# Float64 weights to float32 in an attention and mixture-of-experts kernel: one more ScalarE pass, one fewer VectorE pass, half of the residuals moved from GpSimd to VectorE

## The chip, the cores and the metric

The kernel runs on one core of a Trainium2 chip. The metric is the device time of one execution in microseconds (us). Engines have the names of the profile: PE is TensorE's matrix multiply and PEld its weight load, DVE is VectorE, ACT is ScalarE, POOL is GpSimd, SP is SyncE, which issues most of the transfers (DMAs).

## The reference

Three steps follow one another. All tokens are 4 batches of 448, with a model width of 768.

```
q, k = rmsnorm(q, g_q), rmsnorm(k, g_k)                    # 4 batches, 12 heads, 448 tokens, 64 wide
x = softmax(q @ k.T / 8) @ v                                # then 1792 tokens x 768
x = (sigmoid(x @ w_gate) * (x @ w_val)) @ w_out             # w: 768x1536, 768x1536, 1536x768, float64
e = argmax(normalised(x) @ normalised(expert_emb).T / tau)  # 8 experts, one per token
out = gate * (relu(x @ w1[e]) @ w2[e])                      # w1: 768x1024, w2: 1024x768
```

The weights of the second step (`moe_w_gate`, `moe_w_val`, `moe_w_out`) come in as float64. The chip gets their bytes as pairs of 32-bit words and must itself make float32 numbers of them. That conversion is what changes here.

## The kernel before, in words

Attention goes through 24 pairs of heads, six to a batch, in ticks of one tile each: a matmul whose row maxima DVE takes (line 363), the scores (385, 386), their exponentials on ACT (388), sums on POOL (396) and the product with v on PE (411). Beside it runs the second step (`glu`, line 678), one batch behind: for each of 12 column blocks a gate product and a value product on PE (674), ACT's tanh of the first (697), DVE's product of the two (699), and a split of the result in two parts; then six column blocks of `w_out`.

Every weight is used in two parts, so that three fast products give a float32 one: `wh` is the weight rounded by ACT (line 576), `wl` is what is left, `raw - wh`, worked out on an engine that the caller names (579). A weight piece has 128 partitions of 768 numbers. There are 36 pieces: 24 of gate and value in turn, 12 of `w_out`.

The first of the batches (`b == 0`) is the one that converts. A piece comes from HBM as 768 KB of float64 words into a buffer `r64` (the tile `r` of the trace), of which there are two; the SP queue issues that transfer (line 564). Its words are pairs, a low and a high one, so each of the two is read with a step of two words. Before the change ACT multiplies the high word, read as a float32, by 2 to the power of -112, which puts right the exponent (613, into a tile `sq` of its own, two buffers). Three DVE passes then put the float32 together: a shift left by three (615), the three top bits of the low word put in (617), the sign put in (619):

```
nc.scalar.activation(sq, fv(high), AF.Copy, scale=REBIAS)
nc.vector.tensor_single_scalar(m, sq.bitcast(I32), 3, op=ALU.logical_shift_left)
nc.vector.scalar_tensor_tensor(out=m, in0=low, scalar=29, in1=m, ...)
nc.vector.scalar_tensor_tensor(out=m, in0=sq.bitcast(I32), scalar=-0x80000000, in1=m, ...)
```

The finished float32 piece is written to a scratch tensor (620), from which the later batches read it, and split into `wh` and `wl` for this batch. In this stage `wl` is always made on POOL.

What sets the order: each engine runs its instructions in the order of its own queue. The feed of weights is a Python generator (`feed`, line 550) that is advanced step by step between attention's ticks, one step to each of its yields, at most two pieces ahead of the one in use (LEAD) and with two fetches under way (FETCH). A planner with a modelled timeline then orders the instructions on each engine by these priorities and by when buffers come free. So a feed pass that has to wait holds up all that stands behind it on its engine, attention's instructions too. A fetch into `r64` waits until the last reader of the piece two before it is done; before the change that is line 617.

Of the kernel before, what the change touches and what calls it, by code (L numbers as in the profile page):

```python
# [10 lines left out]
F32 = mybir.dt.float32  # L11
F32R = mybir.dt.float32r
BF16 = mybir.dt.bfloat16
I32 = mybir.dt.int32
U32 = mybir.dt.uint32
AF = mybir.ActivationFunctionType
ALU = mybir.AluOpType
# [12 lines left out]
P = 128  # L30
# [40 lines left out]
SQB = 2  # L71
# [18 lines left out]


REBIAS = 2.0 ** -112


def fv(ap):
    return ap.bitcast(F32)
# [3 lines left out]
def tile_kernel(ctx, tc, q, k, v, g_q, g_k, w_gate, w_val, w_out, emb, tau, w1, w2, out):  # L100
    nc = tc.nc
    cp = ctx.enter_context(tc.tile_pool(name="cp", bufs=1))
    wp = ctx.enter_context(tc.tile_pool(name="wp", bufs=3))
# [446 lines left out]
    def feed(todo, k):  # L550

        def fetch(k, b, at, src, n):
            if at == "raw":

                tag = next(places)
                raw = wp.tile([P, n, P], F32, tag=tag, name=f"wr{k}", bufs=SQB if tag == "sq64" else 3)
                nc.sync.dma_start(raw, src)
                return [raw], None
            raw = [wp.tile([P, n, src.shape[-1] if b is None else P], F32, tag=("wr", "sq64")[i], name=f"wr{k}_{i}", bufs=(3, SQB)[i])
                   for i in range(len(at or "1"))]  # L560
            r64 = None
            if b == 0:
                r64 = wp.tile([P, n, 2 * P], I32, tag="r64", name=f"r64{k}", bufs=2)
                nc.sync.dma_start(r64, src)
            elif b is None:
                nc.sync.dma_start(raw[0], src)
            else:
                for r, i in zip(raw, at):
                    nc.sync.dma_start(r.rearrange("p c f -> p (c f)"), w32[i])
            return raw, r64  # L570

        def split(raw, n, name, eng=nc.vector, small=False):
            tile_ = lambda tag: gp.tile([P, n, P], F32R, tag="rows", name=f"{tag}{name}", bufs=2) if small else \
                wp.tile([P, n, raw.shape[-1]], F32R, tag=tag, name=f"{tag}{name}")
            hi = tile_("wh")
            nc.scalar.copy(hi, raw)  # L576
            yield
            lo = tile_("wl")
            eng.tensor_tensor(lo, raw, fv(hi), ALU.subtract)  # L579
            return [(hi[:, c], lo[:, c]) for c in range(n)]  # L580

        ahead = []
        beside = iter((1,) * NBES)
        places = iter(PLACES)

        def more():
            for p in islice(todo, 1):
                with tc.issue_after(last["rows"]) if "rows" in last else nullcontext():
                    ahead.append((fetch(k + len(ahead), *p), p))

        for _ in range(FETCH):
            more()
        while ahead:
            (raw, r64), (b, at, src, n) = ahead.pop(0)
            k += 1
            if len(raw) == 2:
                fed.append((yield from sums(k - 1, *raw, split)))
                more()
                yield
                continue  # L600
            raw = raw[0]
            if at == "raw":
                fed.append(raw)
                more()
                yield
                continue
            if r64 is not None:


                word = r64.rearrange("p c (f t) -> p c f t", t=2)  # L610
                low, high = word[:, :, :, 0], word[:, :, :, 1]
                sq = wp.tile([P, n, P], F32, tag="sq64", name=f"sq64{k - 1}", bufs=SQB)
                nc.scalar.activation(sq, fv(high), AF.Copy, scale=REBIAS)  # L613
                m = raw.bitcast(I32)
                nc.vector.tensor_single_scalar(m, sq.bitcast(I32), 3, op=ALU.logical_shift_left)  # L615
                yield
                nc.vector.scalar_tensor_tensor(out=m, in0=low, scalar=29, in1=m, op0=ALU.logical_shift_right, op1=ALU.bitwise_or)  # L617
                yield
                nc.vector.scalar_tensor_tensor(out=m, in0=sq.bitcast(I32), scalar=-0x80000000, in1=m, op0=ALU.bitwise_and, op1=ALU.bitwise_or)  # L619
                nc.sync.dma_start(w32[at[0]], raw.rearrange("p c f -> p (c f)"))  # L620
                yield

            free = b == 0 or b is None and next(beside, 0)
            fed.append((yield from split(raw, n, k - 1, nc.gpsimd if free else nc.vector)))
            more()
            yield

    def sums(k, a, b, split):


        n = NC_ // 2
        lo, hi = slice(0, n), slice(n, NC_)
        pa = yield from split(a, NC_, f"{k}a")
        yield
        p22 = yield from split(b[:, hi], n, f"{k}b", small=True)
        yield
        nc.vector.tensor_tensor(b[:, hi], b[:, lo], b[:, hi], ALU.add)
        nc.vector.tensor_tensor(b[:, lo], a[:, lo], b[:, lo], ALU.subtract)
        yield
        nc.vector.tensor_tensor(a[:, lo], b[:, hi], a[:, lo], ALU.subtract)  # L640
        nc.vector.tensor_tensor(a[:, hi], a[:, hi], a[:, lo], ALU.subtract)
        yield
        qa = yield from split(a, NC_, f"{k}c")
        yield
        qb = yield from split(b, NC_, f"{k}d", nc.gpsimd)
        return dict(a11=pa[:n], a12=pa[n:], a22=p22, s2=qa[:n], s4=qa[n:], s3=qb[:n], s1=qb[n:])

    feeders = [feed(chain(pieces(), expert_pieces()), 0)]
    used = [0]

# [924 lines left out]
```

## Time and profile before

| what | us |
|---|---|
| median of three runs | 1244.69 (1239.98 to 1245.45) |
| the profiled execution's own time | 1244.2 |
| its span, first to last instruction | 1242.5 |
| PE busy in the span | 1158.2 (93%) |
| DVE busy | 883.0 (71%) |
| ACT busy | 639.2 (51%) |
| POOL busy | 585.5 (47%) |

The span is 1.7 us shorter than the execution, which has that much ahead of the first and behind the last instruction. The 36 conversions begin at 97 us and the last ends before 350 us, so the stretch of 97 to 350 us is called the converting stage in what follows. Busy times count what an instruction takes from start to end, with any wait for a port within it.

### The profile page before, as it was taken

Reading aid. Unit: us, or ns where it says so; the run is one execution under the profiler, and the core shown is the slowest. Engines: PE = TensorE matmul, PEld = TensorE weight load, DVE = VectorE, ACT = ScalarE, POOL = GpSimd, SP = SyncE. Lnnn points to the kernel's source line nnn. Section 1 sums busy time; section 2 is a strip of 40 time slices with the busy share of each in tenths; the row PEclk is TensorE's granted clock in tenths of the full one; section 3 lists DMA queues with packets and bytes.
Section 4 is the critical chain, followed back from the end, with each engine's and each line's share of the span. In section 5 each row is a group of like instructions: output and inputs, shape, how many; then the busy total and the mean of one; then the engine's idle time right before and its main releaser. Section 6 shows DMA issues by size and latency. Waiting matters only on the chain. (4 is left out here: it accounts for less than half of the span.)

```text
span 1242.5 us, 18474 instructions
## 1 busy us (share of the span) xinstructions
PE 1158.2 (93%) x6516; PEld 947.3 (76%) x6517; DVE 883.0 (71%) x1433; ACT 639.2 (51%) x1203; POOL 585.5 (47%) x470
## 2 busy tenths in 40 slices
PE   3998878889899999999897999999998999999996
PEld 2544666667677777776467989999998899999996
DVE  6889998989878676675678985188456555555652
ACT  5888654656555555665554333233212445555553
POOL 4898975777866565565565322033324100111001
PEclk9999998999999999999899999999999899999999
DMA  4113566655643232211122112121254566777763
GB/s 117 60 45 122 175 215 200 204 189 174 217 136 90 86 94 73 87 61 30 41 86 64 61 52 77 39 64 52 76 154 135 179 179 187 236 232 216 217 195 110
DMA packets 151107, 156.15 MB, mean 126 GB/s; under 512 B 6947, under 2 KB 135205, under 8 KB 151010
## 3 DMA queue, kind: packets, MB, share of 16 engines
q1 hardware_dynamic: 148034, 143.07, 37.7%
q0 software_dynamic: 2848, 11.74, 2.7%
q8 instruction: 53, 0.87, 0.3%
q14 instruction: 44, 0.36, 0.1%
q10 hardware_dynamic: 128, 0.11, 0.0%
HBM read 129.74 MB, written 25.91 MB: 125 GB/s over the span
## 5 line engine op out<-in xcount | busy, mean ns | idle before, releaser
L576 ACT CAST wh<-wr 128x768 fp32r<-128x768 f32 (+1 forms) x212 | 171.5, 809 | 180.6 <-DMA wr<-in_w_dram 55.5
L579 DVE TENSOR_TENSOR wl<-wr,wh 128x768 fp32r<-128x768 f32 (+1 forms) x176 | 166.4, 946 | 136.8 <-ACT wh L576 119.3
L363 DVE TENSOR_REDUCE nm<-m 112x1 fp32r<-112x448 f32 x192 | 114.5, 616 | 41.8 <-PE m L362 40.6
L388 ACT ACTIVATE pt<-s 112x448 f32<-112x448 f32 x192 | 102.4, 541 | 61.3 <-PE s L386 56.9
L396 POOL TENSOR_TENSOR sum<-pt,sum 112x448 f32<-112x448 f32 x78 | 106.5, 1374 | 31.7 <-ACT pt L388 31.4
L265 POOL TENSOR_TENSOR ms<-ms,mhalf 112x8 f32<-112x8 f32 x46 | 79.7, 1733 | 50.1 <-ACT ms L264 49.9
L411 PE MATMUL av<-pt,v 112*64 112x448 f32 x384 | 98.0, 582 | 0.8 <-ACT pt L388 0.3
L579 POOL TENSOR_TENSOR wl<-wr,wh 128x768 fp32r<-128x768 f32 x36 | 76.5, 2127 | 28.3 <-ACT wh L576 26.8
L385 PEld LDWEIGHTS s<-X,Y 128*112 128x112 f32 x192 | 34.4, 179 | 69.7 <-issue 58.7
L385 PE MATMUL s<-X,Y 128*112 128x448 f32 x192 | 81.6, 425 | 4.2 <-ACT pt L388 4.2
L362 PE MATMUL m<-Y,X 128*112 128x448 f32 x192 | 72.6, 414 | 13.6 <-ACT X L308 4.8
L396 POOL TENSOR_TENSOR sum<-pt,pt 112x448 f32<-112x448 f32 x48 | 60.2, 1256 | 47.8 <-ACT pt L388 34.3
L1283 POOL DMA_INDIRECT xe<-x2d,iu_all x16 | 18.6, 1163 | 123.0 <-PE pxe L1308 119.5
L386 PE MATMUL s<-X,Y 128*112 128x448 f32 x192 | 72.3, 382 | 2.9 <-ACT X L372 2.9
L613 ACT ACTIVATE sq<-r 128x768 f32<-128x768 f32 x36 | 32.8, 910 | 56.9 <-DMA r<-in_w_out_dram 24.7
L362 PEld LDWEIGHTS m<-Y,X 128*112 128x112 f32 x192 | 35.1, 187 | 33.9 <-DVE nm L363 6.8
L1294 POOL DMA_INDIRECT out_dram<-orow,iu_all x16 | 18.7, 1169 | 89.3 <-ACT orow L1415 79.5
L617 DVE SCALAR_TENSOR_TENSOR wr<-r,wr 128x768 int32<-128x768 int32 x36 | 58.7, 1630 | 0.7
L619 DVE SCALAR_TENSOR_TENSOR wr<-sq,wr 128x768 int32<-128x768 int32 x36 | 58.4, 1624 | 0.4
L674 PE MATMUL ph<-xeh,wh 128*128 128x256 f32 (+2 forms) x336 | 50.3, 284 | 0.0
L674 PE MATMUL ph<-xel,wh 128*128 128x256 f32 (+2 forms) x336 | 49.8, 282 | 0.0
L615 DVE TENSOR_SCALAR wr<-sq 128x768 int32<-128x768 int32 x36 | 40.9, 1137 | 12.0 <-POOL wl L579 6.6
(778 smaller groups left out, 3078.4 us busy)
## 6 DMA issues: line engine op xcount, KB each, us to landing
wr<-in_w_dram SPq DMA_DIRECT2D x112, 384.0 KB, 3.7
wr<-w SPq DMA_DIRECT2D x72, 384.0 KB, 3.1
w<-wr SPq DMA_DIRECT2D x36, 384.0 KB, 3.8
r<-in_w_gate_dram SPq DMA_DIRECT2D x12, 768.0 KB, 4.6
r<-in_w_val_dram SPq DMA_DIRECT2D x12, 768.0 KB, 5.1
r<-in_w_out_dram SPq DMA_DIRECT2D x12, 768.0 KB, 4.9
wr<-in_w_dram SPq DMA_DIRECT2D x24, 256.0 KB, 2.9
v<-in_v_dram SPq DMA_DIRECT2D x24, 224.0 KB, 3.4
```

Of the source, the lines that this page charges most:

```text
L265: nc.gpsimd.tensor_tensor(m, m, mhalf[:CP, :m.shape[1]], ALU.pow)
L362: nc.tensor.matmul(s_[:CP, :S], lhsT=st["X"][j][:, c * CP:(c + 1) * CP], rhs=st["Y"][j][0], start=True, stop=True)
L363: last["max"] = nc.vector.tensor_reduce(st["nm"][:, 2 * c + j:2 * c + j + 1], s_[:CP, :S], axis=AX.X, op=ALU.max, negate=True)
L385: nc.tensor.matmul(s_[:CP, :S], lhsT=yh[:, z], rhs=st["X"][j], start=True, stop=False)
L386: nc.tensor.matmul(s_[:CP, :S], lhsT=yl[:, z], rhs=st["X2"][j], start=False, stop=True)
L388: last["exp"] = nc.scalar.activation(p_, s_[:CP, :S], AF.Exp)
L396: eng.tensor_tensor(st["sum"][j], p_, st["PT"][j, 0] if kc == 1 else st["sum"][j], ALU.add)
L411: beside(*(lambda j=j: nc.tensor.matmul(st["av"][part_of(j), :S], lhsT=st["v"][:, j, kc], rhs=st["PT"][j, kc], start=kc == 0, stop=kc == N ...
L576: nc.scalar.copy(hi, raw)
L579: eng.tensor_tensor(lo, raw, fv(hi), ALU.subtract)
L617: nc.vector.scalar_tensor_tensor(out=m, in0=low, scalar=29, in1=m, op0=ALU.logical_shift_right, op1=ALU.bitwise_or)
L674: nc.tensor.matmul(pt[:, :cols], lhsT=wts[i][a], rhs=xs[i][z], start=first and k == 1, stop=last and k == 3 * n)
```

## The change

Two ACT passes work in place on the words in `r64`. The first reads the low word as an unsigned integer, scales it by 2 to the power of -29 with a small offset and writes the result as an integer, so that rounding leaves the top three bits as a number from 0 to 7. The second rescales the high word, as before, but where it stands. DVE then has two passes: the high word shifted left by three and joined with the small integer, and the sign put in. Both read `r64`; the tile `sq` is gone. And `wl` of the first batch's pieces goes to DVE and POOL in turn: the piece counter starts at one, so odd pieces (the gates among the first 24) go to DVE and even ones to POOL, 18 each.

```
+STEP = 2.0 ** -20
+THREE = dict(scale=2.0 ** -29 * (1 - STEP), bias=7.5 * STEP - 0.5)
+WL = "PD"
...
-                sq = wp.tile([P, n, P], F32, tag="sq64", name=f"sq64{k - 1}", bufs=SQB)
-                nc.scalar.activation(sq, fv(high), AF.Copy, scale=REBIAS)
+                nc.scalar.activation(low, low.bitcast(U32), AF.Copy, **THREE)
+                nc.scalar.activation(fv(high), fv(high), AF.Copy, scale=REBIAS)
+                yield
                 m = raw.bitcast(I32)
-                nc.vector.tensor_single_scalar(m, sq.bitcast(I32), 3, op=ALU.logical_shift_left)
+                nc.vector.scalar_tensor_tensor(out=m, in0=high, scalar=3, in1=low, op0=ALU.logical_shift_left, op1=ALU.bitwise_or)
                 yield
-                nc.vector.scalar_tensor_tensor(out=m, in0=low, scalar=29, in1=m, op0=ALU.logical_shift_right, op1=ALU.bitwise_or)
-                yield
-                nc.vector.scalar_tensor_tensor(out=m, in0=sq.bitcast(I32), scalar=-0x80000000, in1=m, op0=ALU.bitwise_and, op1=ALU.bitwise_or)
+                nc.vector.scalar_tensor_tensor(out=m, in0=high, scalar=-0x80000000, in1=m, op0=ALU.bitwise_and, op1=ALU.bitwise_or)
                 nc.sync.dma_start(w32[at[0]], raw.rearrange("p c f -> p (c f)"))
                 yield
...
-            free = b == 0 or b is None and next(beside, 0)
+            free = b == 0 and WL[k % len(WL)] == "P" or b is None and next(beside, 0)
             fed.append((yield from split(raw, n, k - 1, nc.gpsimd if free else nc.vector)))
```

The number of yields to a piece stays at five.

## Rows read from the trace of the kernel before

**Rows 1.** Busy time by stretch: busy us and instructions per engine, clock, DMA.

```profile
core 0: us, PE busy (x) PEld busy (x) DVE busy (x) ACT busy (x) POOL busy (x), PEclk, DMA share, GB/s
0.00:97.00 97.00, 75.95 (x333) 38.64 (x334) 79.09 (x146) 71.67 (x153) 72.68 (x85) 1.00 0.25 74
97.00:350.00 253.00, 217.58 (x1000) 158.65 (x998) 234.24 (x252) 148.21 (x265) 198.41 (x131) 0.96 0.56 185
380.00:640.00 260.00, 255.25 (x1250) 181.60 (x1247) 182.97 (x302) 153.26 (x298) 157.68 (x123) 0.98 0.23 72
350.00:1242.50 892.50, 864.66 (x5187) 750.05 (x5187) 569.72 (x1038) 419.28 (x786) 314.45 (x256) 0.99 0.38 115
```

**Rows 2.** PE's waits from 97 to 350 us: total, times, longest.

```profile
PE pv L674 <- DVE sg L699: 9.0, 4, 5.0
PE pg L674 <- ACT sg L697: 4.7, 3, 3.6
PE rb L428 <- DVE nm L363: 3.7, 3, 2.6
PE m L362 <- DVE Y L352: 2.6, 1, 2.6
PE pg L674 <- DVE xh L315: 2.6, 2, 2.0
PE pk L344 <- DVE rt L433: 2.1, 1, 2.1
PE m L362 <- DVE nm L363: 1.7, 1, 1.7
PE s L385 <- ACT pt L388: 1.6, 1, 1.6
```

**Rows 3.** DVE's costliest groups, 97 to 350 us: busy, mean ns, idle before.

```profile
L617 DVE SCALAR_TENSOR_TENSOR wr<-r,wr 128x768 int32<-128x768 int32 x36 | 58.7, 1630 | 0.7
L619 DVE SCALAR_TENSOR_TENSOR wr<-sq,wr 128x768 int32<-128x768 int32 x36 | 58.4, 1624 | 0.4
L615 DVE TENSOR_SCALAR wr<-sq 128x768 int32<-128x768 int32 x36 | 40.9, 1137 | 12.0 <-POOL wl L579 6.6 <-ACT sq L613 5.1 <-issue 0.2
```

**Rows 4.** The same lines alone: ns min/median/max, first and last start.

```profile
L615 DVE TENSOR_SCALAR wr<-sq x36: 496/560/4849, 98.9 to 342.8; 128x768 int32<-128x768 int32 x36
L617 DVE SCALAR_TENSOR_TENSOR wr<-r,wr x36: 936/1086/3562, 100.8 to 344.7; 128x768 int32<-128x768 int32 x36
L619 DVE SCALAR_TENSOR_TENSOR wr<-sq,wr x36: 908/1294/5034, 104.7 to 347.2; 128x768 int32<-128x768 int32 x36
```

**Rows 5.** Timeline around 162 us, DVE and POOL: start, us.

```profile
161.80 4.85 DVE L615 TENSOR_SCALAR wr<-sq 128x768 int32<-128x768 int32 x1
...
164.44 1.79 POOL L579 TENSOR_TENSOR wl<-wr,wh 128x768 fp32r<-128x768 f32 x1
```

**Rows 6.** POOL's costliest group, 97 to 350 us.

```profile
L579 POOL TENSOR_TENSOR wl<-wr,wh 128x768 fp32r<-128x768 f32 x35 | 74.6, 2135 | 28.3 <-ACT wh L576 26.8 <-PE pg L674 1.5
```

**Rows 7.** DVE's group of the same operation, 380 to 640 us.

```profile
L579 DVE TENSOR_TENSOR wl<-wr,wh 128x768 fp32r<-128x768 f32 x33 | 35.3, 1069 | 7.9 <-ACT wh L576 3.5 <-PE pg L674 3.1 <-ACT pt L388 1.1
```

**Rows 8.** ACT's costliest group, 97 to 350 us.

```profile
L613 ACT ACTIVATE sq<-r 128x768 f32<-128x768 f32 x36 | 32.8, 910 | 56.9 <-DMA r<-in_w_out_dram 24.7 <-DMA r<-in_w_gate_dram 19.1 <-DMA r<-in_w_val_dram 11.2
```

**Rows 9.** Timeline, 197 to 199 us, with the idle time ahead.

```profile
197.36 0.89 ACT L613 ACTIVATE sq<-r 128x768 f32<-128x768 f32 x1 [7.20 <-DMA r<-in_w_gate_dram]
...
198.34 0.56 DVE L615 TENSOR_SCALAR wr<-sq 128x768 int32<-128x768 int32 x1 [3.60 <-ACT sq L613]
```

**Rows 10.** Busy time by stretch again, columns as in rows 1.

```profile
200.00:215.00 15.00, 14.37 (x53) 11.02 (x53) 14.70 (x14) 7.95 (x13) 11.73 (x7) 0.78 0.49 169
```

**Rows 11.** SP's wait for buffers of weight words, 97 to 350 us.

```profile
SPq L564 <- DVE wr L617: 121.2, 32, 7.3
```

**Rows 12.** Timeline of SP: the fifth and the thirty-first fetch.

```profile
128.36 0.39 SPq L564 DMA_DIRECT2D r<-in_w_gate_dram  x1
...
293.68 0.37 SPq L564 DMA_DIRECT2D r<-in_w_out_dram  x1
```

**Rows 13.** The tile of weight words: its transfers from issue to landing.

```profile
DMA to landing us min/median/max: 4.2/4.9/8.1
```

## The prediction, made before the changed kernel ran

> **What bounds the kernel now.** I read the busy time by stretch first. From 350 us on PE is busy for 864.7 of 892.5 us [rows 1]: nothing that the change touches lies there, and there is little to win. The change works from 97 to 350 us. There PE is busy for 217.6 of 253 us, so it stands idle for 35.4; DVE is busy for 234.2 (93%), POOL for 198.4 (78%), ACT for 148.2 (59%). The stage is bound by DVE, with PE waiting on it now and then. The stretch of 380 to 640 us is the comparison: attention runs there too, DVE is at 70%, and PE is busy for 255 of 260 us. So time won in the converting stage should stay won.
>
> Second, whom PE waits for [rows 2]. The eight largest waits name DVE for 9.0 + 3.7 + 2.6 + 2.6 + 2.1 + 1.7 = 21.7 us and ACT for 4.7 + 1.6 = 6.3 us. None of these waits is for a weight; they are for DVE's product of gate and value, maxima and copies, and ACT's tanh: short instructions that come late because of what stands ahead of them in their queue. Two waits are traced further. The 5.0 us wait: DVE had stood 3.60 us for the ACT pass of line 613, and that pass 7.20 us for its words from HBM [rows 9]. The 3.6 us behind ACT is of the same kind, as line 613's idle time is nearly all DMA [rows 8].
>
> Third, what fills DVE. The three conversion passes take 58.7 + 58.4 + 40.9 = 158.0 of its 234.2 us [rows 3]. Their shortest are 0.94, 0.91 and 0.50 us [rows 4]; all 36 of each at that would be 84 us. The other 74 us is waiting inside the instruction: the 4.85 us case began in the middle of a run of POOL instructions and ended as the 1.79 us one did [rows 5].
>
> Fourth, the feed. SP waited 121 us in 32 fetches for line 617 to free an r64 buffer [rows 11]. From the fifth fetch to the thirty-first, 26 pieces, takes 165.3 us [rows 12], 6.36 us a piece, and with two buffers 12.7 us of holding each.
>
> **The change, part by part.**
>
> *The shift pass goes.* 36 x 1.137 us = 40.9 us off DVE [rows 3].
>
> *The two joining passes stay, with other operands.* The first now reads both inputs with a step of two words, the second one. Line 617 read one such input and line 619 none, and their shortest differ by 0.03 us [rows 4], so I take no change; the other end is a rival below. The Trainium skill speaks against this ("Vector Engine (DVE) Microarchitecture Reference", section "Measured stream behaviour on trn2"): a stream runs at full rate only in runs of two or more adjacent words, and one source that hops at every element costs 1.73 ns a column. By that line 617 would take over 768 x 1.73 ns = 1.33 us, an estimate from the page's figure; its shortest, 0.94 us [rows 4], decides against the rule for one input a step of two apart, and two such inputs no row shows.
>
> *Half of wl moves to DVE.* 18 x 1.07 us = 19.2 us, the duration from the stage where DVE already does it beside a POOL that is busy for 61% [rows 7, 1]; after the change POOL would be at (198.4 - 18 x 2.135) / 253 = 63% [rows 6]. The upper end is 18 x 1.63 = 29.3 us, what a two-input pass takes now beside POOL [rows 3]. DVE must also wait for wh: 7.9 / 33 = 0.24 us each there, so 4.3 us, and at most what POOL waits now, 18 x 28.3 / 35 = 14.6 us [rows 6, 7].
>
> *POOL gets shorter by 38.4 us* and blocks DVE less. The joining passes lose 117.1 - 36 x (0.94 + 0.91) = 50.5 us to waiting; with a fifth less POOL work I take 9.7 us off, with nothing and 20 us as the ends. What stood behind those wl on POOL (sums, scaled q and k) comes earlier, which nothing waits for much.
>
> DVE in sum: -40.9 + 19.2 + 4.3 - 9.7 = -27 us, which leaves it occupied for 207 of 253 us (82%). The ends are -40.9 + 29.3 + 14.6 = +3 and, with wl at the 0.94 us of the shortest two-input pass and no wait for wh, -40.9 + 17 - 20 = -44.
>
> *What PE gets of it.* Without the 5.0 us that a transfer caused, 16.7 us of PE's idle time lies behind DVE's queue. At 93% it is that; at 70% (380 to 640 us) PE loses under 5 us to everything. 82% is half way, and waiting in a queue falls faster than its load, so I take 0.6: -10.0 us (ends 0 and -16.7).
>
> *ACT gets 36 more passes.* 36 x 0.91 = 32.8 us [rows 8], 148 to 181 us, 72%. They lie in its idle time, which is 105 us. But exponentials and tanh queue behind them: the 6.3 - 3.6 = 2.7 us that PE waits for ACT without DMA grows with ACT's load by 22%, +0.6 us (ends 0, and one pass ahead of each of the four waits, +3.6).
>
> *The r64 buffers and SP's queue.* The fetch of piece k + 2 now waits for the second joining pass, not the first. Holding changes by +0.91 (ACT) + 1.62 (second pass) - 1.14 (shift pass) = +1.4 us, 0.7 us a piece, if nothing else moves. Against it: of the 12.7 us, 4.9 are the transfer [rows 13], 0.91 + 0.50 + 0.94 the passes, and some 5.5 us waiting in DVE's queue and for POOL; 26% less of that (and of the same behind the second pass) pays for the 1.4 us. I take it as even: 0. The scratch store, behind the same pass, and the loads of q, k and v queue around the fetch in SP, which has nothing else to do; one issue of 0.37 us can come ahead of the fetch.
>
> *sq goes.* Of line 613's 56.9 us of idle time 55.0 is DMA [rows 8]; the 1.9 us left is the most that sq's two buffers can have cost ACT, and I take 0.
>
> *Clock.* The granted clock is 0.96 in the stage [rows 1], the full 2.4 GHz level but for stretches at 1.2 GHz: 0.04 x 253 = 10.1 us of full-speed work lost. Right after the 5.0 us gap 200 to 215 us has 0.78 [rows 10]. With fewer gaps I take 0.4 of it back, -4.0 us (ends 0 and -10.1).
>
> Sum: -10.0 + 0.6 - 4.0 = -13.4 us on the profiled 1244.2, so 1230.8; that execution is 0.5 us under the median of the runs, so **1231 us**. With every term at its end it lies between 1244.7 + 3.6 = 1248 and 1244.7 - 16.7 - 10.1 = 1218.
>
> **The rivals.**
>
> *The two r64 buffers become the bound, and it gets slower.* Place: the fetch that waits for the second joining pass. For it: SP already waits for the buffer at nearly every fetch [rows 11], and ACT for words 55 us in the stage [rows 8]; an ACT that stands before a transfer holds back tanh and exponentials. Against it: the holding time is mostly DVE's queue, which shortens. It decides if DVE's part of the holding shrinks by less than 26%. Price: 0.7 us for each of the 24 gate and value pieces, which PE uses as they come, 17 us, less half of the 10 us won on DVE: 1244.7 + 12 = **1257 us**.
>
> *PE's gaps are set by transfers and by the order, not by DVE's load: no change.* DVE is relieved but waits instead, at the head of its queue, for ACT and HBM or for wh, as in rows 9. For it: the largest two gaps (8.6 us) are of that kind. Then -5 us of gaps and +3.6 us of ACT: **1243 us**.
>
> *The step-of-two inputs cost.* Should a second such input add as much as POOL adds to line 617 today, 1.63 - 0.94 = 0.69 us, that is +25 us on DVE and leaves 2 of the 27: **1243 us**. By the Trainium skill's rule above both passes would take about 1.4 us, some 34 us more on DVE, and the saving would be gone altogether.
>
> *DVE's relief frees more.* All 21.7 us behind DVE goes, as a shorter holding brings the words earlier, and with the gaps most of the clock loss: 1244.7 - 21.7 - 9 = **1214 us**. For it: the stage after, where PE hardly waits. Against it: the longer chain from words to weight.
>
> *The change does not do what it says:* if the planner puts the two ACT passes or DVE's wl where their inputs come late, the count of instructions holds but their waits grow; that is in the no-change case.
>
> **How the numbers follow.** Forecast 0.47, more freed 0.10, no change 0.21, strided inputs 0.06, r64 0.16. A measurement of this kernel can tell about 0.5% (6.2 us) from no change: bounds 1238.5 and 1250.9. Faster: 0.10, nearly all of the forecast (0.44) and a little of the no-change cases (0.04), 0.58. Slower: 0.16. Same: 0.26. The range goes from 1215, just inside the case of more freed, to 1253, which takes in the mildest part of the r64 case and leaves out the rest of both, under 0.2.
>
> **What would show it.** Right: line 615 gone; two DVE passes of about 1.4 us; 18 residuals on DVE of 1.0 to 1.3 us; ACT's two passes 0.9 us each; DVE at 80 to 84% of a stage some 13 us shorter; the DVE names among PE's waits at 10 us or less; the clock above 0.96; the rest of the span as it was. Wrong: fetches more than 6.4 us apart and PE's waits under ACT's tanh or DVE's product longer (r64); joining passes whose shortest is over 1.2 us (strided inputs); DVE idle before wl (the order).

## The result, and the profile after

The changed kernel takes 1213.2 us (median of four runs, 1212.62 to 1215.77) against 1244.66 of the kernel before: a ratio of 0.9759 (95% interval 0.9731 to 0.9787). The forecast was 1231, its range 1215 to 1253; the time lies 1.8 us below the range, in the case "DVE's relief frees more" (1214). The profiled execution took 1212.88 us, its span 1211.1, so the 31.3 us can be read off two traces.

One instruction serves as a mark in both: ACT's cast `wh72b` of a weight piece, a few casts behind the last float64 one. It starts at 379.55 us before and at 356.07 us after, and PE first uses it at 663.3 and 635.3 us. The next two fences cut the span there, before and after (busy time by stretch, columns as in rows 1).

```profile
0.00:379.50 379.50, 322.75 (x1483) 219.66 (x1486) 330.92 (x428) 236.92 (x452) 289.29 (x232) 0.97 0.48 153
379.50:663.30 283.80, 275.90 (x1354) 197.42 (x1355) 202.83 (x328) 164.37 (x322) 168.83 (x134) 0.98 0.23 71
663.30:1242.50 579.20, 559.53 (x3684) 530.26 (x3682) 349.29 (x679) 237.87 (x431) 127.42 (x106) 0.99 0.45 134
```

```profile
0.00:356.00 356.00, 319.34 (x1480) 214.56 (x1481) 287.98 (x409) 263.94 (x488) 261.15 (x214) 0.98 0.52 163
356.00:635.30 279.30, 272.58 (x1357) 196.45 (x1356) 204.28 (x330) 163.57 (x321) 171.04 (x134) 0.99 0.23 73
635.30:1211.10 575.80, 557.86 (x3683) 528.83 (x3682) 349.10 (x678) 237.55 (x431) 125.43 (x106) 0.99 0.45 135
...
97.00:350.00 253.00, 238.44 (x1127) 173.77 (x1126) 207.12 (x258) 190.27 (x331) 183.59 (x125) 0.97 0.63 200
97.00:328.00 231.00, 216.64 (x1013) 156.06 (x1012) 192.34 (x234) 175.19 (x300) 171.20 (x114) 0.97 0.65 206
```

PE does the same work in each part (1483 and 1480 matmuls, 1354 and 1357, 3684 and 3683). The parts are 23.5, 4.5 and 3.4 us shorter. In the first, PE's idle time falls from 56.75 to 36.66 us, by 20.1, and its busy time by 3.4. In the two behind, busy time falls by 3.3 and 1.7 us and idle time by 1.2 and 1.7. The fall in busy time is the clock: up to PE's last matmul the trace's clock records have 41.0 us at the 1.2 GHz level before and 23.9 after, which at half speed is 8.5 us of full-speed work, and PE's busy time fell by 8.4 in all. So of 31.4 us of span, 23.0 are gaps of PE that closed, nearly all in the converting stage, and 8.4 are the clock, of which 5.0 lie behind that stage.

The last row shows the stage without what has moved up into it: the last joining pass now starts at 323.3 us, so 97 to 328 us answers to 97 to 350 of [rows 1] within some 3 us. DVE's work there went from 234.2 to 192.3 us, ACT's from 148.2 to 175.2, POOL's from 198.4 to 171.2. Next, all of PE's waits from 97 to 350 us after the change, to set beside [rows 2]:

```profile
PE pg L680 <- ACT sg L703: 3.6, 3, 2.3
PE s L391 <- ACT pt L394: 2.8, 2, 1.5
PE s L392 <- ACT X L378: 2.3, 1, 2.3
PE pq L309 <- DVE nm L369: 1.4, 2, 1.0
PE pm L375 <- DVE nm L369: 1.3, 1, 1.3
PE m L368 <- ACT Y L321: 1.1, 2, 0.7
PE pt_en L150 <- DVE emt L146: 0.7, 1, 0.7
PE pg L680 <- ACT wh L582: 0.5, 1, 0.5
PE pv L680 <- DVE sg L705: 0.2, 1, 0.2
PE px L994 <- DVE nm L369: 0.2, 1, 0.2
```

This is the whole list, and [rows 2] has only the eight largest of before. Nine smaller ones follow them there, four of them behind ACT:

```profile
PE s L386 <- ACT X L372: 1.5, 1, 1.5
...
PE m L362 <- ACT Y L315: 0.9, 2, 0.7
...
PE m L362 <- ACT rows L993: 0.7, 1, 0.7
...
PE av L411 <- ACT pt L388: 0.3, 1, 0.3
```

With these, ACT's names come to 9.7 us before and 10.3 after. DVE's come to 24.6 before (21.7 in the eight rows, 2.9 in four smaller ones) and 3.8 after; the wait for the product of gate and value, 9.0 us then, is 0.2. So the waits behind DVE went and those behind ACT stayed. ACT is now the one that PE waits for, in gaps of at most 2.3 us. The groups of DVE, POOL and ACT in the same stretch (columns as in rows 3), and the two joining passes alone (as in rows 4):

```profile
L625 DVE SCALAR_TENSOR_TENSOR wr<-r,wr 128x768 int32<-128x768 int32 x36 | 54.2, 1506 | 0.5
L623 DVE SCALAR_TENSOR_TENSOR wr<-r 128x768 int32<-128x768 int32 x36 | 41.1, 1141 | 24.6 <-ACT r L620 20.9 <-issue 2.5 <-POOL wl L585 1.0
...
L585 DVE TENSOR_TENSOR wl<-wr,wh 128x768 fp32r<-128x768 f32 x21 | 24.2, 1154 | 7.1 <-ACT wh L582 5.9 <-PE po L680 1.1
...
L585 POOL TENSOR_TENSOR wl<-wr,wh 128x768 fp32r<-128x768 f32 x18 | 37.0, 2056 | 20.7 <-ACT wh L582 20.7
...
L619 ACT ACTIVATE r<-r 128x768 int32<-128x768 uint32 x36 | 33.0, 916 | 23.8 <-DMA r<-in_w_out_dram 10.5 <-DMA r<-in_w_gate_dram 7.6 <-DMA r<-in_w_val_dram 5.7
L582 ACT CAST wh<-wr 128x768 fp32r<-128x768 f32 x39 | 32.5, 834 | 22.2 <-DVE wr L625 20.7 <-POOL rsq L1004 1.3
L620 ACT ACTIVATE r<-r 128x768 f32<-128x768 f32 x36 | 32.3, 897 | 0.0
...
L623 DVE SCALAR_TENSOR_TENSOR wr<-r x36: 941/959/2214, 100.1 to 322.1; 128x768 int32<-128x768 int32 x36
L625 DVE SCALAR_TENSOR_TENSOR wr<-r,wr x36: 939/1332/2926, 105.4 to 323.3; 128x768 int32<-128x768 int32 x36
```

The joining passes cost 95.3 us, where [rows 3] has 117.1, though each now reads a strided input: they wait less inside. ACT's wait for words from HBM is 23.8 us, from 55.0 [rows 8]; in its place ACT waits 20.7 us for DVE's finished piece (the cast; 13.9 before), and DVE 20.9 for ACT's second pass (the first conversion pass of before waited 5.1 for ACT [rows 3]). The feed of float64 pieces, fifth and thirty-first fetch:

```profile
132.49 0.37 SPq L570 DMA_DIRECT2D r<-in_w_gate_dram  x1
...
285.95 0.39 SPq L570 DMA_DIRECT2D r<-in_w_out_dram  x1
```

That is 153.5 us for 26 pieces, 5.90 us each, against 6.36 [rows 12].

### The profile page after: what moved, and what is told of

Read it like the earlier page. It is cut to its first block, busy times and chain, and to the rows that moved or that the text cites. A ratio compares the mean times of both kernels' runs of the same rounds, so it can differ in the third digit from the quotient of the medians.

```text
span 1211.1 us, 18407 instructions
## 1 busy us (share of the span) xinstructions
PE 1149.8 (95%) x6516; PEld 939.8 (78%) x6517; DVE 841.4 (69%) x1415; ACT 665.1 (55%) x1239; POOL 557.6 (46%) x452
## 5 line engine op out<-in xcount | busy, mean ns | idle before, releaser
L585 DVE TENSOR_TENSOR wl<-wr,wh 128x768 fp32r<-128x768 f32 (+1 forms) x194 | 188.5, 972 | 142.1 <-ACT wh L582 123.5
L369 DVE TENSOR_REDUCE nm<-m 112x1 fp32r<-112x448 f32 x192 | 114.2, 615 | 33.2 <-PE m L368 31.3
L271 POOL TENSOR_TENSOR ms<-ms,mhalf 112x8 f32<-112x8 f32 x46 | 85.6, 1860 | 36.6 <-ACT ms L270 36.4
L623 DVE SCALAR_TENSOR_TENSOR wr<-r 128x768 int32<-128x768 int32 x36 | 41.1, 1141 | 24.6 <-ACT r L620 20.9
L625 DVE SCALAR_TENSOR_TENSOR wr<-r,wr 128x768 int32<-128x768 int32 x36 | 54.2, 1506 | 0.5
L680 PE MATMUL ph<-xeh,wl 128*128 128x256 f32 (+2 forms) x336 | 49.4, 282 | 0.0
L585 POOL TENSOR_TENSOR wl<-wr,wh 128x768 fp32r<-128x768 f32 x18 | 37.0, 2056 | 20.7 <-ACT wh L582 20.7
L709 POOL TENSOR_TENSOR gl<-sg,gh 128x448 fp32r<-128x448 f32 x24 | 33.0, 1374 | 29.4 <-DVE gh L321 22.1
```

Of the source, the lines that this page charges most:

```text
L271: nc.gpsimd.tensor_tensor(m, m, mhalf[:CP, :m.shape[1]], ALU.pow)
L369: last["max"] = nc.vector.tensor_reduce(st["nm"][:, 2 * c + j:2 * c + j + 1], s_[:CP, :S], axis=AX.X, op=ALU.max, negate=True)
L625: nc.vector.scalar_tensor_tensor(out=m, in0=high, scalar=-0x80000000, in1=m, op0=ALU.bitwise_and, op1=ALU.bitwise_or)
L680: nc.tensor.matmul(pt[:, :cols], lhsT=wts[i][a], rhs=xs[i][z], start=first and k == 1, stop=last and k == 3 * n)
```

## The experiments

Two theories stood against each other. By the first the change is load: less work on DVE, and less waiting inside DVE's instructions with POOL emptier. By the second it is the buffers and the order: the words are held until the second joining pass, the planner sees that, and puts ACT's and DVE's queues in another order. The expectations divide them further: theory A is DVE's load, B the waiting that POOL causes inside DVE's passes, C the buffers as what paces the stage, D the planned order as the later release makes it, E any other order, L the length of the loop from fetch to release. All runs of one group of kernels shared their runs of the kernel before, so ratios compare best; "mark" is the start of `wh72b` in the one profiled execution of each (before 379.6, after 356.1 us), and "PE there" is PE's first use of `wh72b`, which has the same 2835 matmuls ahead of it in every trace (before 663.3 us).

| kernel | median us | ratio to before (95%) | mark us | PE there us |
|---|---|---|---|---|
| after, first runs | 1213.2 | 0.9759 (0.9731 to 0.9787) | 356.1 | 635.3 |
| after_again | 1212.87 | 0.9774 (0.9747 to 0.9802) | 356.5 | 634.3 |
| conv_only | 1228.62 | 0.9881 (0.9842 to 0.9919) | 370.2 | 648.6 |
| wl_only | 1233.68 | 0.9909 (0.9873 to 0.9944) | 375.2 | 653.9 |
| all_dve | 1209.13 | 0.9730 (0.9701 to 0.9758) | 351.8 | 628.8 |
| all_dve_again | 1208.17 | 0.9736 (0.9708 to 0.9765) | 351.7 | 628.2 |
| after_sq | 1232.83 | 0.9907 (0.9877 to 0.9937) | 368.0 | 651.9 |
| after_sq_hold | 1217.70 | 0.9798 (0.9781 to 0.9816) | 359.8 | 636.1 |
| before_hold | 1237.08 | 0.9945 (0.9926 to 0.9965) | 381.8 | 658.9 |
| wl_hold | 1228.10 | 0.9905 (0.9868 to 0.9941) | 367.9 | 648.1 |
| after_dp | 1219.89 | 0.9804 (0.9773 to 0.9835) | 362.6 | 640.4 |
| after_shift | 1234.43 | 0.9932 (0.9912 to 0.9952) | 378.1 | 654.8 |
| after_shift_out | 1229.61 | 0.9864 (0.9829 to 0.9899) | 374.4 | 652.0 |
| after_act | 1239.21 | 0.9987 (0.9967 to 1.0008) | 381.7 | 659.9 |
| after_act_out | 1228.27 | 0.9855 (0.9820 to 0.9889) | 368.3 | 652.8 |

### Each part alone

conv_only has the new conversion, with every residual of the stage on POOL; wl_only has the old conversion with the residuals in turn:

```
conv_only, against after:        wl_only, against before:
-WL = "PD"                       +WL = "PD"
+WL = "P"                        -  free = b == 0 or ...
                                 +  free = b == 0 and WL[k % len(WL)] == "P" or ...
```

> The conversion changed alone, all of wl on POOL as before. Theory A (what counts is time off DVE's queue, and PE's waits behind DVE fall with it): DVE loses the shift pass, 41 us, and some waiting, and takes on no wl, so nearly the whole gain comes from here: 1214 to 1222 us, PE's waits behind DVE in the converting stage under 6 us. Theory B (POOL's occupation of the shared port is what hurts): POOL is as full as before, the joining passes still take 1.6 us each, and half of the gain or less comes: 1228 us or more. Theory C (the r64 buffers pace the stage): fetches stay 6.3 us apart and the time is 1240 us or more.

> The old conversion with its three DVE passes, half of wl moved from POOL to DVE. Theory A: DVE gains 18 x 1.15 = 21 us and gets 10 to 20 us of waiting back, so nothing moves: 1240 to 1248 us. Theory B: the passes get shorter by more than wl costs, 1225 to 1235 us. Theory C: 1243 to 1247 us.

Both times lie in the range of theory B, and in conv_only the joining passes still take 1.6 us (rows in the next section), as B had it. By the ratios conv_only is 14.8 us faster than before and wl_only 11.3; together 26.1, where both give 28.1 to 30.0. With intervals of some 4.5 us on each, the parts add up as far as this can tell. Ahead of the mark they do not: there the one trace of each has 9.4 us for conv_only and 4.4 for wl_only, and 23.5 for both. Each part alone gains another 5 us between the mark and PE's first use of `wh72b`, and both together gain 4.5 there, so the sum of the parts counts that stretch twice. The two rows of busy time from 97 to 350 us, conv_only and then wl_only:

```profile
97.00:350.00 253.00, 228.72 (x1058) 165.35 (x1059) 205.34 (x229) 184.06 (x320) 205.92 (x138) 0.96 0.60 192
```

```profile
97.00:350.00 253.00, 225.98 (x1025) 165.22 (x1024) 233.18 (x279) 152.73 (x274) 174.01 (x116) 0.95 0.57 190
```

In wl_only DVE is as busy as before (233.2 against 234.2 us), although 18 residuals of 1069 ns were added. The three conversion passes pay for them:

```profile
L619 DVE SCALAR_TENSOR_TENSOR wr<-r,wr 128x768 int32<-128x768 int32 x36 | 53.5, 1487 | 0.5
L621 DVE SCALAR_TENSOR_TENSOR wr<-sq,wr 128x768 int32<-128x768 int32 x36 | 48.4, 1344 | 0.4
L617 DVE TENSOR_SCALAR wr<-sq 128x768 int32<-128x768 int32 x36 | 36.3, 1009 | 9.1 <-POOL wl L581 5.4 <-DMA x2d<-zr 2.1 <-issue 0.8
```

Against [rows 3] that is 36 x (0.143 + 0.280 + 0.128) = 19.8 us less, close to the 19.2 us of residuals. Moving this work from POOL to DVE costs DVE nothing here. That the kernel's gain comes from the shorter POOL fits this, but the order of the queues changed with it, and no run parts the two.

### All residuals on DVE

```
-WL = "PD"
+WL = "D"
```

> The kernel after with all 36 wl of the converting stage on DVE. DVE takes on another 18 x 1.1 = 20 us and POOL loses 37 us, so that POOL blocks DVE less (10 us back or so). Theory A: DVE is about 10 us fuller than after, 1216 to 1224 us. Theory B (POOL's hold on the port is what hurts): the joining passes fall to 1.1 to 1.2 us and it is 1213 us or less.

all_dve was run twice, the second time beside after unchanged:

> The kernel after with all 36 wl on DVE, beside the kernel after on the same chip. If POOL's hold on the port costs DVE more than the work it takes over, as the first run of it suggests (1209 us): 2 to 8 us faster than the kernel after. If that run was chance: within 2 us of it.

> The kernel after, unchanged, as the yardstick of this chip for the runs beside it: 1211 to 1216 us.

all_dve came out as theory B had it in time, and nearly in the joining passes (1.04 and 1.17 us). Its second run took 1208.17 us beside the 1212.87 of after: 4.7 us, 0.4%, within the 2 to 8 us expected. The ranges (1204.93 to 1211.51 and 1209.85 to 1215.02) and the intervals just overlap, but the first group's ratio (0.9730) has it on the same side of after. It is the fastest version here, if by little. Its DVE groups and its stretch from 97 to 350 us, and then the joining passes of conv_only:

```profile
L585 DVE TENSOR_TENSOR wl<-wr,wh 128x768 fp32r<-128x768 f32 x39 | 45.0, 1153 | 6.4 <-ACT wh L582 6.3
L625 DVE SCALAR_TENSOR_TENSOR wr<-r,wr 128x768 int32<-128x768 int32 x36 | 42.0, 1167 | 0.4
L623 DVE SCALAR_TENSOR_TENSOR wr<-r 128x768 int32<-128x768 int32 x36 | 37.6, 1044 | 21.6 <-ACT r L620 21.2
```

```profile
97.00:350.00 253.00, 237.59 (x1142) 174.87 (x1140) 209.06 (x278) 191.14 (x334) 155.72 (x110) 0.99 0.63 200
```

```profile
L625 DVE SCALAR_TENSOR_TENSOR wr<-r,wr 128x768 int32<-128x768 int32 x36 | 57.2, 1589 | 0.6
L623 DVE SCALAR_TENSOR_TENSOR wr<-r 128x768 int32<-128x768 int32 x36 | 56.9, 1579 | 34.0 <-ACT r L620 11.1 <-POOL wl L585 9.2 <-issue 5.5
```

From conv_only over after to all_dve POOL's busy time goes 205.9, 183.6, 155.7 us, and the two joining passes go from 1579 and 1589 ns over 1141 and 1506 to 1044 and 1167. DVE's busy time stays at 205.3, 207.1 and 209.1, while the mark moves from 370.2 over 356.1 to 351.8 us. So DVE's busy time alone doesn't order these kernels: a busy microsecond of conv_only holds more waiting. This also agrees with the Trainium skill ("SBUF — State Buffer", section "Who interferes with whom"): a DVE instruction with two inputs in SBUF contends with a GpSimd one that reads there. The shift pass of before, with one input, waits too [rows 4, 5], which that sentence does not cover.

### When the words are released

before_hold lets the third pass of before read the sign from the words in `r64` instead of `sq`, so that the buffer is held to the end; wl_hold is the same edit on wl_only. after_sq does the reverse on after: the rescaled high word goes into a tile of its own again, so that the first joining pass is the last reader of `r64`. after_sq_hold then differs from after_sq in one operand.

```
before_hold, wl_hold, third pass:   after_sq, against after:
-  in0=sq.bitcast(I32)              -  nc.scalar.activation(fv(high), fv(high), ...)
+  in0=high                         +  sq = wp.tile([P, n, P], F32, tag="sq64", ..., bufs=SQB)
                                    +  nc.scalar.activation(sq, fv(high), ...)
after_sq_hold, against after_sq:    first and second joining pass:
second joining pass                 -  in0=high
-  in0=sq.bitcast(I32)              +  in0=sq.bitcast(I32)
+  in0=high
```

> The kernel before, with the third pass reading the sign from the word in r64 and not from sq, so that r64 is held until the end of the third pass, about 2.3 us longer; every other instruction is the same. Theory C (the buffers pace the stage): 36 pieces x 1.1 us, 1265 us or more. Theory A: the fetch comes later but DVE's queue sets the pace, and the transfer is hidden behind it: 1244 to 1252 us.

> The kernel after, with the rescaled high word written to a tile of its own again, so that r64 is free after the first joining pass, some 1.5 to 2 us earlier, and the second pass reads no word with a step. Theory C: fetches come closer together and it is faster by 5 us or more, under 1208 us. Theory A: DVE's queue is unchanged, 1211 to 1215 us.

> As the run with the tile sq (1232.8 us), but the second joining pass takes the sign from the word in r64, so that r64 is again held until that pass ends; all instructions are of the same kinds, durations and engines as in the kernel after. Theory D (when r64 comes free sets where the planner puts the ACT passes and the fetches, and that, not DVE's load, makes the last 19 us): about 1213 us, with ACT's wait for words back from 37 to about 24 us. Theory E (any other edit of this size shifts the planned order as much, and 1213 is one draw of it): anywhere from 1211 to 1235 us, most likely near 1228.

> The old conversion with half of wl on DVE, and r64 held until the third pass. Theory D (holding keeps the planner from running conversions ahead, and pays once DVE has room): DVE still has three passes and 19 us of wl, so it is full, and holding gives little: 1228 to 1236 us, with the second of the stages starting no more than 4 us earlier than in the run with half of wl moved alone. If holding is worth its 15 us everywhere: under 1222 us.

before_hold (1237.1) and after_sq (1232.8) fell into no range of their expectations, after_sq_hold into the wide one of E, 4.7 us above D's time. after_sq has all of the change's loads and is only 11.6 us faster than before; held to the end, the same instructions are 25.1 us faster (0.9907 against 0.9798, 13.6 us by the ratios). The one trace of each agrees: after_sq_hold is 8.2 us ahead at the mark and 15.8 at PE's first use of `wh72b`. The pair also moves the release of `sq` one pass earlier. No ACT pass waits for `sq` in either trace, but the planner reads that release too, so what is shown is the effect of the two together. Its presence matters little: after_sq_hold, which has the tile `sq`, and after differ by 0.2 to 0.4%, with overlapping intervals. Their rows of the stretch, and of ACT's first pass, after_sq and then after_sq_hold:

```profile
97.00:350.00 253.00, 226.73 (x1070) 164.10 (x1069) 203.86 (x250) 185.30 (x321) 170.15 (x123) 0.96 0.59 195
...
L619 ACT ACTIVATE r<-r 128x768 int32<-128x768 uint32 x36 | 33.0, 917 | 39.1 <-DMA r<-in_w_out_dram 13.7 <-DMA r<-in_w_gate_dram 11.9 <-DMA r<-in_w_val_dram 11.2
```

```profile
97.00:350.00 253.00, 234.33 (x1113) 171.94 (x1112) 210.98 (x256) 188.33 (x328) 174.50 (x123) 0.98 0.63 200
...
L619 ACT ACTIVATE r<-r 128x768 int32<-128x768 uint32 x36 | 32.9, 915 | 23.8 <-DMA r<-in_w_out_dram 12.1 <-DMA r<-in_w_val_dram 7.3 <-DMA r<-in_w_gate_dram 4.1
```

PE stands idle for 26.3 of the 253 us in after_sq and 18.7 in after_sq_hold, where before has 35.4 [rows 1] and after 14.6. The kernel that releases early isn't short of words: its fetches come every 5.70 us, those of after_sq_hold every 6.08. What differs is the order on ACT. Counted in the traces, 29 first passes stand ahead of the twelfth tanh in after_sq, as in before and in wl_only, and they run up to three or four pieces ahead of the casts; with the buffer held it is 26 (in after, all_dve and before_hold too) and one piece ahead. A first pass that stands early waits for its transfer (36.8 us against 23.5) with tanh, exponentials and casts behind it. That the order is what the 13.6 us come from is argued from this; the trace doesn't show it wait by wait, since ACT's idle time ahead of the casts grows as its wait for words shrinks (2.4 to 22.1 us).

Nor is it a rule that holding pays this much. before_hold gains 0.55%, but its mark comes 2 us later than in before and its gain lies wholly behind the mark, although 26 first passes stand ahead of the twelfth tanh there too. wl_hold is no faster than wl_only by the ratios; in the one trace of each its mark comes 7.3 us earlier, where its expectation allowed 4. So the size of what holding gives there stays open. A second case of another order with the same work is after_dp, in which even pieces go to DVE instead of odd ones:

```
-WL = "PD"
+WL = "DP"
```

> The kernel after with the halves swapped: odd pieces' wl on POOL, even ones' on DVE. The load of every engine is the same. Theory A (DVE's load decides): 1211 to 1217 us. Theory E (the planned order decides as much): 1220 us or more, with another set of PE waits.

Its median is 7 us above that of after, between the ranges of A and E; the intervals overlap, so the size isn't settled. POOL's share is as in after, and yet two DVE groups hold more waiting, 1671 and 1532 ns against 1506 and 1154:

```profile
L625 DVE SCALAR_TENSOR_TENSOR wr<-r,wr 128x768 int32<-128x768 int32 x36 | 60.2, 1671 | 0.6
...
L585 DVE TENSOR_TENSOR wl<-wr,wh 128x768 fp32r<-128x768 f32 x20 | 30.6, 1532 | 4.0 <-ACT wh L582 3.9
```

So how busy POOL is doesn't set that waiting alone; it also depends on what the order puts side by side.

### What one more pass costs

Four kernels add 36 passes that the result doesn't need. after_shift and after_act put one into the conversion, where it also lengthens the holding of `r64`; the two others put it behind the split, on the finished piece, into a scratch tile.

```
after_shift:      +  nc.vector.tensor_single_scalar(m, high, 3, op=ALU.logical_shift_left)
after_act:        +  nc.scalar.activation(fv(high), fv(high), AF.Copy, scale=1.0)
after_shift_out:  +  nc.vector.tensor_single_scalar(sx.bitcast(I32), raw.bitcast(I32), 3, op=...)
after_act_out:    +  nc.scalar.activation(sx, raw, AF.Copy, scale=1.0)
```

> The kernel after with the old shift pass put back in front of the first joining pass, which writes over its result: 36 more passes of about 1.1 us on DVE, some 41 us, and nothing else. Theory A: DVE is as full as before the change and nearly all of the gain in the converting stage goes, 1232 to 1242 us. Theory E or D (the order is what gained): under 1225 us.

> The kernel after with one more ACT pass on each piece, times one, between the rescale and the first joining pass: 36 x 0.90 = 32 us more on ACT and nothing on DVE. If ACT's added pass was free, as the forecast has it within 0.6 us: 1212 to 1218 us. If ACT's queue is now what holds PE (its waits behind ACT were 10 us in the kernel after): 1220 us or more.

> The kernel after with the extra shift pass on DVE behind the split, from the finished piece to a tile that nothing reads: 36 passes of 0.8 to 1.1 us on DVE, outside the loop. Theory A (DVE's load): 1228 us or more, PE's waits behind DVE back above 12 us. Theory L (the loop alone): 1220 us or less.

> The kernel after with the same extra ACT pass on each piece, but behind the split, from the finished piece to a tile that nothing reads: as much work on ACT, nothing in the loop that holds r64. If the extra pass inside cost 26 us because it lengthened the loop (Theory L): 1212 to 1220 us, fetches 6.0 us apart. If because ACT was full: 1230 us or more.

Against after (0.9759 and 0.9774) the pass outside costs 11 to 13 us on DVE and 10 to 12 on ACT, with intervals of some 4 us on each; inside it costs 20 to 22 and 26 to 28. after_shift came out as theory A had it, and after_act shows that the added pass was not free. after_shift_out lies in A's range by time, but PE's waits behind DVE stay under A's 12 us (8.6); after_act_out, at 1228.3 us, lies between its two ranges. Two things follow. ACT isn't an engine with room to spare: a pass of 0.8 us costs about as much there as one of 0.9 us on DVE. And the chain from fetch to release seems near to being the bound, as far as these four runs tell: fetches come 6.85 us apart in after_shift and 7.14 in after_act, against 6.29 and 6.54 with the pass outside. In after_act PE begins to wait for the weights themselves (its first rows of waits):

```profile
PE po L681 <- ACT wh L582: 7.5, 6, 2.0
PE pg L681 <- ACT wh L582: 7.0, 6, 1.7
PE pv L681 <- ACT wh L582: 5.6, 5, 3.6
```

In after that wait was 0.5 us. after_shift_out puts DVE's load back to where it was:

```profile
97.00:350.00 253.00, 227.86 (x1046) 164.85 (x1046) 235.14 (x277) 179.08 (x309) 180.59 (x118) 0.96 0.59 187
```

With 235.1 us on DVE, before's 234.2, it is still 17 us faster than before by the ratio (0.9864). By this the DVE load that the change took off is worth 11 to 13 us at this point, less than half of the gain.

## Why the prediction was wrong, point by point

*What bounds the kernel.* Right in place: 23.5 of 31.4 us came out of the converting stage, and PE's waits on DVE went. Too narrow in cause: wl_only gains 11.3 us with DVE just as busy, so POOL's length or the order counted as well.

*The shift pass, -40.9 us, and half of wl, +19.2.* Right: line 615 is gone, and 18 residuals at 1154 ns are 20.8 us. The wait for `wh`, put at 4.3, is 5.9.

*Joining passes with a step of two.* Right: the shortest with two such inputs is 941 ns, with one 939, against 936 and 908 in [rows 4]. The rival falls, and for a step of two words the price falls with it that the Trainium skill ("Vector Engine (DVE) Microarchitecture Reference", section "Measured stream behaviour on trn2") gives for a source that hops 4 KiB at every element, 1.73 ns a column: 941 ns for 768 columns are 1.23.

*POOL gets shorter, -9.7 us.* Mis-sized: the joining passes lost 21.8 us (117.1 to 95.3), just past the 20 us that was set as its end, and wl_only has 15.2 by itself (19.8 with the shift pass). DVE's busy time in sum went down by 40.9 + 21.8 - 20.8 = 41.9 us, as the rows have it (234.2 to 192.3), where the three terms of the forecast give 31.4 (27 with the wait for `wh`).

*What PE gets of it, -10.0 us.* The step was too low, by its base and by its 0.6: PE's waits behind DVE fell by 20.8 us (24.6 to 3.8), and its idle time up to the mark by 20.1. The base left out 2.9 us in the smaller rows, and the 5.0 us gap. That gap was set aside as caused by a transfer; it is gone too. As I read it now, it hung on a transfer only because the order had put a first pass there in ACT's queue, and that order was not fixed.

*The r64 buffers, "I take it as even: 0".* **This is the step that failed.** I priced the later release as a longer holding and looked for which of two durations was longer. The planner reads the release when it orders the queues, and the later one gave another order, worth 13.6 us here (after_sq against after_sq_hold), in the other direction from the rival I had built on it. Without it the change gives 11.6 us, close to the 13.4 of the forecast's sum. That closeness is partly luck: PE's idle time in the stage falls by 9.1 us in after_sq (35.4 to 26.3), where the forecast had -10.0 and +0.6, but from waits behind DVE that fall by 14.0 (24.6 to 10.6) and waits behind ACT that grow by 4.3 (9.7 to 14.0). The rival isn't empty: after_act comes near the loop as the bound, one ACT pass further on.

*The rival "DVE's relief frees more".* The time fell into it, and its terms came out nearly: 20.8 us behind DVE where it had 21.7, and 8.4 of clock where it had 9. Its reason, a shorter holding that brings the words earlier, is not enough: two buffers at 5.90 us a piece are 11.8 us of holding against 12.7, but after_sq has 11.4 and only 11.6 us of gain.

*ACT gets 36 more passes, +0.6 us.* The number came out, 9.7 to 10.3 us over all the rows, but not as the price of a pass in idle time: with the early release the same passes cost 4.3 (after_sq), past the end of +3.6, and a further pass outside the loop costs 10 to 12.

*Clock, -4.0 us.* Right in the stage (-3.4). "The rest of the span as it was" was not: it is 7.9 us shorter behind the mark, 5.0 by the clock. Why is open. The same time behind the mark varies from 851.5 to 863 us over these kernels, 855.0 and 851.6 in two executions of after itself, and follows none of the edits. What varies lies mostly ahead of PE's first use of `wh72b`; from there on every one of the sixteen traces takes 573.9 to 579.3 us.

Left open, then: how much each of load and order gives in the step from before to after. The prices above are taken at after's load and don't sum to the whole, and it wasn't tried to give two kernels the same order by hand.

## What to carry to other kernels

Where a planner orders the queues, a change of a buffer's last reader is a change of order: look for which instructions it lets be placed early, and price it as unknown in both directions, not as a difference of two holding times. A pass with two inputs in SBUF beside a busy POOL holds waiting that a shorter POOL can give back, in wl_only as much as the moved work cost, so compare the shortest with the mean before costing a move. And an engine at 59 to 76%, as ACT before and after, that short instructions of the critical path pass through is not free.

## What the runs showed of the hardware

Two inputs with a step of two words cost DVE nothing against one: 941 and 939 ns at the shortest for 128 x 768, with none 908. An ACT pass from unsigned to signed integers, in place and with that step, takes 916 ns, where the float one takes 897. And the same two-input pass took 1579, 1141 or 1044 ns on the mean while POOL was busy for 205.9, 183.6 or 155.7 of 253 us; after_dp shows that the order counts there too.
